# Attention with two mixtures of experts on one core: exponentials last in ScalarE's step, one scatter per step, a drain written out by hand

## The chip, the cores and the metric

The kernel runs on one core of a Trainium2 chip. The metric is the device time of one execution in microseconds (us), the median of several runs; the profile is of one further execution of the same program.

## The reference

Attention in a window of 128 positions with a linear bias per head, then a mixture of eight experts in which each token goes to the expert of its largest logit, then a mixture of four experts that every token visits:

```python
# q, k, v: 4 x 8 heads x 576 x 64
scores = q @ k.T / sqrt(64) + slope[head] * -abs(rel)      # rel = query position - key position
mask = (rel >= 0) & (rel < 128)
attn = softmax(where(mask, scores, -1e9)); x = attn @ v    # -> 2304 rows of 512
# mixture 1: 8 experts, w1 512x1024, w2 1024x512
e = argmax(x @ w_gate); x = gate[e] * relu(x @ w1[e]) @ w2[e]
# mixture 2: 4 experts
out = sum_e p[:, e] * (relu(x @ w1[e]) @ w2[e])
```

## The kernel before

The 2304 rows are 18 tiles of 128 (`NTT`). **Attention** goes over 36 steps s (`ns`), two per tile: step s handles tile t = s // 2 and four of its eight heads. It is a pipeline of three steps' depth, and everything is issued in the order in which the Python loop of lines 700 to 753 writes it; each engine takes its own instructions in that order. In step s:

- `st_qk(s)`: TensorE writes the bias (L418) and the scores (L426, each operand in a high and a low part) of this step.
- `st_max(s)`: ScalarE copies half the scores out (L436), VectorE takes the maximum with the other half (L437) and the row maxima `nm` (L442).
- `st_turn(s-2)`: TensorE transposes the probabilities of two steps ago (L459), ScalarE copies them to SBUF (L461), GpSimd cuts them into two triangles (L468: the window's part in this tile and in the one before).
- `st_exp(s)`: ScalarE takes four exponentials (L449), which wait for `nm`.
- `st_vw(t)` in odd steps: TensorE multiplies the values by the gate's weights (L540).
- `st_pv(s-3)`: TensorE multiplies the triangles by the values (L480, 16 matmuls); `st_row(s-3)`: VectorE divides by the sums (L505 to L527), and after a tile's second half adds up the gate's logits (L552).
- then the splits of coming keys and queries into high and low parts (`split_k`, `split_q`: ScalarE L246 or L258, VectorE L247 or L259), builds of two further bias tables in the first eleven steps (L304, ScalarE, up to three per step), and in six of the steps the high and low part of one weight tile (L134 on ScalarE, L138 on VectorE in the next step).

**Routing** is done by groups of tiles (`CUTS`: 0-2, 3-5, 6-8, 9-11, 12-13, 14-15, 16, 17). When a group's logits are there, a generator (`st_route`) is queued in `back`; each call of `route_op` issues its next small piece. VectorE finds the expert of each row (L573 to L588), TensorE counts the ranks (L593 to L599; the `yield "rank"` holds it back for the head of a step), VectorE makes the row numbers (L610), and GpSimd scatters each tile's rows to DRAM with an indirect DMA (L625), all tiles of a group one after the other. A second generator (`gates`, from `gate_of`) makes the gate's softmax in five pieces, ahead of any later group. The groups below `LATE` (tiles 0 to 15) are the early ones. After the last of them the first expert's rows so far are read back as `early` (L633). Tiles 16 and 17 reach the first expert by matmuls with a placement matrix (`put`, L653) instead.

The **drain** is three further turns of the same loop: s = 36, 37 and 38 issue the last transposes and products; in turn 38 the rest of tile 16's routing and the transposes of the first `early` tile (`first_rows(0)`, L644) stand ahead of the last product. `first_chunk` then adds the other early tiles, tiles 16 and 17, and splits the result (L185) for the first expert.

The **two mixtures** follow, from the first matmul in L789 to the end.

Of the kernel before, what the change touches and what calls it, by code (L numbers as in the profile page):

```python
# [14 lines left out]
ALU = mybir.AluOpType  # L15
# [35 lines left out]
def kernel(  # L51
# [153 lines left out]
    def attention():  # L205
        actx = ExitStack()
        with actx:
# [94 lines left out]
            def build_bias(x, h, o, w):  # L302
                slope = 2.0 ** (-8.0 * (h + 1) / H)
                nc.scalar.activation(  # L304
                    out=biases[x][:, h, o:o + w], in_=rels[x][:, 0:w], func=AF.Copy, scale=-slope
                )
# [253 lines left out]
            def st_route(g):  # L560
# [29 lines left out]
                if t0 < LATE:  # L590
                    yield "rank"
# [32 lines left out]
                for j, t in enumerate(tiles):  # L624
                    nc.gpsimd.indirect_dma_start(  # L625
# [32 lines left out]
            def first_chunk():  # L658
                first_rows(1, 2)
# [27 lines left out]
            held = []  # L687

            def route_op(rank=False):
                todo = gates if gates and (not back or gates[0][0] < back[0][0]) else back  # L690
                if not todo or (held and not rank):
                    return
                held.clear()
                got = next(todo[0][1], "end")
                if got == "end":
                    todo.pop(0)
                elif got == "rank":
                    held.append(todo)

            for s in range(ns + 3):  # L700
# [5 lines left out]
                if s < ns:  # L706
                    st_qk(s)
                    if s == 1:
                        busy(ps_t, "t", 4)
                    st_max(s)  # L710
                if 2 <= s < ns + 2:
                    st_turn(s - 2)
                if s < ns:
                    st_exp(s)
                route_op(rank=True)
                if s == ns + 2:
                    while back:
                        route_op(rank=True)
                    first_rows(0)
                if hf == 1 and s < ns:  # L720
                    st_vw(t)
# [3 lines left out]
                if s == ns + 2:  # L725
                    break
# [3 lines left out]
                if s < ns:  # L730
                    if hf == 0:
                        if 2 <= t + 1 < NTT:
                            split_k(t + 1)
                        if t + 3 < NTT:
                            load(t + 3)
                    elif t + 2 < NTT:
# [651 lines left out]
```

## Time and profile before

| what | us |
|---|---|
| median of 3 runs (1188.45 to 1192.49) | 1188.8 |
| the profiled execution | 1188.37 |
| its span in the trace | 1185.7 |
| attention's steps 5 to 34 | 24.60 to 166.94 |
| step 35 and the drain, up to the first expert's first matmul | 166.94 to 194.86 |
| the two mixtures | 194.86 to 1185.7 |

To read it: TensorE is busy for nearly all of the span, so what counts is its clock and the time between its matmuls. "PEclk" is the granted clock of TensorE as a share of the full one: 1.00 is 2.4 GHz all the time, and a stretch at 1.2 GHz counts half. A table by stretches gives for each engine the busy time and the number of instructions. In a timeline each row is a start, a duration, an engine, a source line, an operation and its tiles; a bracket tells how long the engine had been idle before it and who ended the wait. A name with a prefix of a queue (SPq) is a DMA's issue.

### The profile page before, as it was taken

The numbers are of one execution on the slowest core, as the hardware profiler recorded it, in microseconds if no ns is written. First come the engines' busy times: TensorE is split into PE (matmuls) and PEld (weight loads), VectorE is DVE, ScalarE is ACT, GpSimd is POOL, SyncE is SP. The second block draws the span as 40 slices with busy tenths as digits, with TensorE's granted clock in tenths as the row PEclk, the third lists the DMA queues.
The fourth block names the chain that finished last, engine by engine and source line by source line (L and its number), as shares of the span: only waits on it lengthen the run. The fifth ranks groups of instructions, "written<-read, shape, count | busy, mean of one in ns | idle before, by whom it ended". The sixth has DMA issues, their size and how long they took to land.

```text
span 1185.7 us, 17746 instructions
## 1 busy us (share of the span) xinstructions
PE 1157.8 (98%) x6785; PEld 1057.4 (89%) x6786; DVE 773.0 (65%) x1428; ACT 527.5 (44%) x988; POOL 112.3 (9%) x158
## 2 busy tenths in 40 slices
PE   8999997999999999999999999999999999999997
PEld 5787887999999998999999899999999899999996
DVE  4678774465575466666666876666667866666663
ACT  5776652454465453333333443333334433333331
POOL 3244341001310000000000100000000200000001
PEclk9799898999999999999999999999999999999999
DMA  9556423455575413211122322112212322222201
GB/s 328 189 162 213 157 76 126 154 191 168 156 216 166 141 44 101 65 57 59 70 72 71 103 93 72 63 63 71 72 58 67 125 72 71 71 72 71 72 18 53
DMA packets 62225, 126.58 MB, mean 107 GB/s; under 512 B 26272, under 2 KB 26272, under 8 KB 62112
## 3 DMA queue, kind: packets, MB, share of 16 engines
q1 hardware_dynamic: 58368, 114.96, 30.5%
q0 software_dynamic: 3456, 9.51, 2.0%
q8 instruction: 79, 1.29, 0.5%
q10 hardware_dynamic: 288, 0.52, 0.1%
q14 instruction: 34, 0.28, 0.1%
HBM read 109.18 MB, written 15.80 MB: 105 GB/s over the span
## 4 chain that ended last, share of the span: by engine, by line
issue 71%; PE 20%; POOL 3%; DVE 3%; ACT 2%; DMA 1%; POOLq 0%; ACTq 0%; SPq 0%; DVEq 0%
PE g L789 6%; PE y L894 6%; PE xo L480 3%; PE sc L426 2%; POOL out_dram L1319 2%; ACT pr L449 1%; PE pt L459 1%; PE sc L418 1%; DVE nm L442 1%; PE vw L540 1%; POOL pt L468 1%; DVE pr L437 1%; PE xps L861 1%; POOL xs L625 0%; ACT pr L436 0%
## 5 line engine op out<-in xcount | busy, mean ns | idle before, releaser
L138 DVE TENSOR_TENSOR wlo<-raw,whi 128x1024 fp32r<-128x1024 f32 x160 | 193.4, 1221 | 130.1 <-ACT whi L134 128.5
L1298 PE MATMUL l<-whi,hhi 128*128 128x512 f32 x576 | 224.5, 390 | 1.6 <-DVE acc L1315 1.6
L1298 PE MATMUL l<-whi,hlo 128*128 128x512 f32 x576 | 224.9, 390 | 0.0
L1298 PE MATMUL l<-wlo,hhi 128*128 128x512 f32 x576 | 224.8, 390 | 0.0
L134 ACT CAST whi<-raw 128x1024 fp32r<-128x1024 f32 x160 | 165.4, 1053 | 130.9 <-DVE raw L160 106.0
L1211 ACT COPY x<-X 128x384 f32<-128x384 f32 x126 | 60.4, 480 | 269.2 <-PE X L1190 269.2
L1315 DVE SCALAR_TENSOR_TENSOR acc<-l,ct,acc 128x512 f32<-128x512 f32 x126 | 94.2, 748 | 81.7 <-PE l L1298 81.7
L1298 PEld LDWEIGHTS l<-whi,hhi 128*128 128x128 f32 x576 | 108.2, 188 | 24.4 <-DVE acc L1315 2.5
L1298 PEld LDWEIGHTS l<-whi,hlo 128*128 128x128 f32 x576 | 108.2, 188 | 22.5
L1298 PEld LDWEIGHTS l<-wlo,hhi 128*128 128x128 f32 x576 | 108.2, 188 | 21.9
L1319 POOL DMA_INDIRECT out_dram<-acc,ctok x18 | 22.2, 1236 | 818.0 <-DVE acc L1315 488.2
L1216 DVE TENSOR_TENSOR x<-Z,x 128x384 f32<-128x384 f32 x84 | 44.7, 554 | 67.5 <-ACT x L1211 67.5
L480 PE MATMUL xo<-vr,pt 128*128 128x73 f32 x544 | 74.4, 292 | 3.6 <-POOL pt L468 2.0
L480 PEld LDWEIGHTS xo<-vr,pt 128*128 128x128 f32 x544 | 69.6, 206 | 5.9 <-POOL pt L468 5.9
L1222 ACT ACTIVATE hhi<-x 128x384 fp32r<-128x384 f32 x126 | 58.1, 520 | 30.9 <-DVE x L1216 30.9
L894 PE MATMUL y<-hhi,whi 128*128 128x256 f32 (+2 forms) x224 | 69.7, 311 | 1.0 <-issue 1.0
L894 PE MATMUL y<-hlo,whi 128*128 128x256 f32 (+2 forms) x224 | 69.1, 309 | 0.0
L894 PE MATMUL y<-hhi,wlo 128*128 128x256 f32 (+2 forms) x224 | 68.9, 307 | 0.0
L1228 DVE SCALAR_TENSOR_TENSOR hlo<-x,hhi 128x384 fp32r<-128x384 f32 x126 | 62.8, 553 | 2.7
L449 ACT ACTIVATE pr<-pr,nm 128x128 f32<-128x128 f32 x128 | 40.9, 390 | 39.1 <-DVE nm L442 39.1
L777 ACT ACTIVATE hhi<-g 128x384 fp32r<-128x384 f32 x64 | 31.1, 492 | 49.8 <-PE g L789 45.0
L778 DVE SCALAR_TENSOR_TENSOR hlo<-g,hhi 128x384 fp32r<-128x384 f32 x64 | 35.1, 554 | 27.3 <-ACT hhi L777 23.7
(354 smaller groups left out, 2595.1 us busy)
## 6 DMA issues: line engine op xcount, KB each, us to landing
raw<-in_w_b_dram SPq DMA_DIRECT2D x96, 512.0 KB, 3.6
raw<-in_w_a_dram SPq DMA_DIRECT2D x64, 512.0 KB, 3.8
xs<-zrow SPq DMA_DIRECT2D x8, 768.0 KB, 6.4
row<-xs SPq DMA_DIRECT2D x7, 768.0 KB, 5.5
rk<-in_k_dram SPq DMA_DIRECT2D x18, 256.0 KB, 4.2
vr<-in_v_dram SPq DMA_DIRECT2D x18, 256.0 KB, 3.4
rv<-in_vt_dram SPq DMA_DIRECT2D x18, 256.0 KB, 3.4
rq<-in_q_dram SPq DMA_DIRECT2D x16, 256.0 KB, 4.4
```

The costliest lines, as they stand in the source:

```text
L134: nc.scalar.copy(out=hi, in_=src)
L138: nc.vector.tensor_tensor(out=lo, in0=src, in1=hi.bitcast(F32), op=ALU.subtract)
L449: nc.scalar.activation(out=pr[:, r, jj, :], in_=scores[:, r, jj, :], func=AF.Exp, bias=nm[:, r, jj:jj + 1], scale=1.0,)
L480: nc.tensor.matmul(xo[:, i, :], pt[c][:, i, :], vr[:, c % NSLOT, 4 * hf + i, :], start=(n == 0), stop=(n == len(pt) - 1),)
L789: nc.tensor.matmul(ps[:, 0:w], wl[:, c0:c0 + P], xl[dt // 2][:, dt % 2, 0:w], start=(dt == 0 and n == 0), stop=(dt == NDT - 1 and n == 2),)
L894: nc.tensor.matmul(acc[:, 0:w], wl[:, c0:c0 + P], hl[:, 0:w], start=(f == 0 and x == 0), stop=(f == NFT - 1 and x == 2),)
L1211: nc.scalar.copy(out=to, in_=xb[i])
L1222: nc.scalar.activation(out=hi, in_=c, func=AF.Relu)
L1228: nc.vector.scalar_tensor_tensor(out=lo, in0=c, scalar=0.0, in1=hi.bitcast(F32), op0=ALU.max, op1=ALU.subtract)
L1298: nc.tensor.matmul(acc, hl[:, ts], wl[:, c0:c0 + DM], start=(m == 0 and x == 0), stop=(m == 3 and x == 2),)
L1315: nc.vector.scalar_tensor_tensor(out=accs[g], in0=acc, scalar=pe, in1=accs[g], op0=ALU.mult, op1=ALU.add)
L1319: nc.gpsimd.indirect_dma_start(out=outv[g], out_offset=bass.IndirectOffsetOnAxis(ap=ctok[:, g, :], axis=0), in_=accs.pop(g), in_offset=Non ...
```

## The change

It moves work in attention's loop and in the drain; nothing that is computed changes.

1. `st_exp(s)` is issued behind the splits of keys and queries and the bias builds instead of ahead of them, though still ahead of a weight tile's high part. The builds of the two further tables for odd heads go to VectorE (12 of 40; eight of 128x256 or 128x128 elements for one table, four of 128x256 for the other).
2. The generator of a group stops ("hold") ahead of the rank matmuls, as before, and also ahead of each scatter, and goes on at the head of a step, behind that step's transposes and triangles. Groups of two tiles hold once for both scatters, and the last early group does not hold there.
3. The gate's softmax is issued only while the group's generator holds, or when there is none.
4. The last early group (tiles 14 and 15): its pieces up to the hold are all issued in step 34, and in step 35 the rank matmuls and the next piece, with the scatters and the reads of `early`, follow at once.
5. The drain is written out. The last transposes, products and routing pieces stand in their own order, the rest of tile 16's routing ahead of the last product, and all transposes of `early` (`first_rows(0, 1, 2)`) behind it.

```diff
             def build_bias(x, h, o, w):
...
+                if x and h % 2:
+                    nc.vector.tensor_scalar(out=out, in0=rels[x][:, 0:w], scalar1=-slope, scalar2=None, op0=ALU.mult)
+                else:
+                    nc.scalar.activation(out=out, in_=rels[x][:, 0:w], func=AF.Copy, scale=-slope)
...
                 if t0 < LATE:
-                    yield "rank"
+                    yield "hold"
...
                 for j, t in enumerate(tiles):
+                    if t0 < OPEN and (j == 0 or m > 2):
+                        yield "hold"
                     nc.gpsimd.indirect_dma_start(
...
             def first_chunk():
-                first_rows(1, 2)
+                first_rows(*range(TT))
...
+            def route_op(head=False):
+                if gates and not head and (waiting or not back):
+                    if next(gates[0][1], "end") == "end":
+                        gates.pop(0)
+                elif back and (head or not waiting):
+                    waiting.clear()
+                    got = next(back[0][1], "end")
+                    if got == "end":
+                        back.pop(0)
+                    elif got == "hold":
+                        waiting.append(got)
+
+            for s in range(ns):
...
+                if s >= 2:
                     st_turn(s - 2)
-                if s < ns:
-                    st_exp(s)
-                route_op(rank=True)
...
+                route_op(head=True)
+                if s == 2 * LATE + 3:
+                    route_op()
...
                 route_op()
+                st_exp(s)
                 if late:
                     late.pop(0)()
                 if s in SPLITS:
                     w_split(late)
                 route_op()
+                while s == 2 * LATE + 2 and not waiting:
+                    route_op()
+            st_turn(ns - 2)
+            st_pv(ns - 3)
+            st_row(ns - 3)
+            for _, steps in gates:
+                for _ in steps:
+                    pass
+            st_turn(ns - 1)
+            for _ in range(4):
+                route_op()
+            st_pv(ns - 2)
+            st_row(ns - 2)
+            while back:
+                route_op(head=True)
+            st_pv(ns - 1)
+            st_row(ns - 1)
```

ScalarE in steps 6 and 7 (`pr` are the probabilities, `pt` the transposed ones, `khi` and `qhi` the keys' and queries' high parts), before:

```order
L436 COPY pr_561<-sc_546 128x512
L461 COPY pt_571<-pt_566 128x512
L449 ACTIVATE pr_561<-pr_561,nm_564 128x128 x4
L246 CAST khi<-rk_332 128x4x128
L304 ACTIVATE bias_179<-rel_161 128x256 x3
L134 CAST whi_609<-raw_403 128x1024
L436 COPY pr_627<-sc_612 128x512
L461 COPY pt_637<-pt_632 128x512
L449 ACTIVATE pr_627<-pr_627,nm_630 128x128 x4
L258 ACTIVATE qhi_669<-rq_470 128x512
L304 ACTIVATE bias_179<-rel_161 128x256 x3
```

and now:

```order
L438 COPY pr_561<-sc_546 128x512
L463 COPY pt_571<-pt_566 128x512
L246 CAST khi<-rk_328 128x4x128
L308 ACTIVATE bias_179<-rel_161 128x256 x2
L451 ACTIVATE pr_561<-pr_561,nm_564 128x128 x4
L134 CAST whi_609<-raw_399 128x1024
L438 COPY pr_627<-sc_612 128x512
L463 COPY pt_637<-pt_632 128x512
L258 ACTIVATE qhi_665<-rq_466 128x512
L308 ACTIVATE bias_179<-rel_161 128x256
L451 ACTIVATE pr_627<-pr_627,nm_630 128x128 x4
```

The exponentials moved behind the split and the bias builds of their step, and of the six builds three went to VectorE.

GpSimd where the first group's three tiles are scattered (L468 and L470 are the triangles, two per step; the names with a higher number are later steps), before:

```order
L468 AFFINE_SELECT pt_0_843<-pt_841 128x512
L468 AFFINE_SELECT pt_1_845<-pt_841 128x512
L625 DMA xs<-xrow_392,row_i 18433x512
L625 DMA xs<-xrow_529,row_i 18433x512
L625 DMA xs<-xrow_662,row_i 18433x512
L468 AFFINE_SELECT pt_0_924<-pt_922 128x512
L468 AFFINE_SELECT pt_1_926<-pt_922 128x512
```

and now:

```order
L470 AFFINE_SELECT pt_0_844<-pt_842 128x512
L470 AFFINE_SELECT pt_1_846<-pt_842 128x512
L470 AFFINE_SELECT pt_0_917<-pt_915 128x512
L470 AFFINE_SELECT pt_1_919<-pt_915 128x512
L629 DMA xs<-xrow_388,row_i 18433x512
L470 AFFINE_SELECT pt_0_986<-pt_984 128x512
L470 AFFINE_SELECT pt_1_988<-pt_984 128x512
L629 DMA xs<-xrow_525,row_i 18433x512
L470 AFFINE_SELECT pt_0_1051<-pt_1049 128x512
L470 AFFINE_SELECT pt_1_1053<-pt_1049 128x512
L629 DMA xs<-xrow_658,row_i 18433x512
```

The three scatters stood ahead of one step's triangles; now each stands behind the triangles of its own step.

GpSimd from step 35 on (the first pair of triangles is that of step 33's probabilities, then those of 34 and 35; the scatters are those of tiles 14, 15 and 16), before:

```order
L468 AFFINE_SELECT pt_0_2499<-pt_2497 128x512
L468 AFFINE_SELECT pt_1_2501<-pt_2497 128x512
L468 AFFINE_SELECT pt_0_2540<-pt_2538 128x512
L468 AFFINE_SELECT pt_1_2542<-pt_2538 128x512
L625 DMA xs<-xrow_2267,row_i 18433x512
L625 DMA xs<-xrow_2406,row_i 18433x512
L468 AFFINE_SELECT pt_0_2592<-pt_2590 128x512
L468 AFFINE_SELECT pt_1_2594<-pt_2590 128x512
L625 DMA xs<-xrow_2523,row_i 18433x512
```

and now:

```order
L470 AFFINE_SELECT pt_0_2498<-pt_2496 128x512
L470 AFFINE_SELECT pt_1_2500<-pt_2496 128x512
L629 DMA xs<-xrow_2254,row_i 18433x512
L629 DMA xs<-xrow_2392,row_i 18433x512
L470 AFFINE_SELECT pt_0_2559<-pt_2557 128x512
L470 AFFINE_SELECT pt_1_2561<-pt_2557 128x512
L470 AFFINE_SELECT pt_0_2588<-pt_2586 128x512
L470 AFFINE_SELECT pt_1_2590<-pt_2586 128x512
L629 DMA xs<-xrow_2537,row_i 18433x512
```

The scatters of the last early group moved ahead of step 34's triangles, one step up.

## Rows read from the trace of the kernel before

**Rows 1.** The page: TensorE's granted clock in 40 slices of the span

```profile
PEclk9799898999999999999999999999999999999999
```

**Rows 2.** Table by stretches: length, each engine's busy time, clock, DMA share, GB/s

```profile
24.60:60.19 35.59, 32.49 (x236) 27.16 (x236) 22.59 (x60) 26.06 (x74) 8.51 (x15) 0.81 0.60 205
60.19:90.66 30.47, 30.06 (x279) 25.77 (x278) 24.42 (x73) 21.84 (x53) 13.60 (x18) 1.00 0.57 174
90.66:115.34 24.68, 23.45 (x220) 20.06 (x220) 19.66 (x60) 16.45 (x42) 8.20 (x11) 1.00 0.66 213
115.34:132.44 17.10, 15.53 (x112) 12.97 (x112) 11.43 (x31) 8.78 (x22) 6.99 (x10) 0.80 0.32 108
132.44:166.94 34.50, 34.04 (x318) 29.20 (x318) 27.58 (x88) 23.56 (x59) 15.29 (x20) 1.00 0.51 160
166.94:194.86 27.92, 20.27 (x141) 18.89 (x141) 15.40 (x64) 7.45 (x21) 9.01 (x12) 0.82 0.18 65
194.86:1185.70 990.84, 979.75 (x5364) 908.93 (x5364) 640.98 (x1033) 410.14 (x685) 42.56 (x38) 1.00 0.29 92
```

**Rows 3.** Timeline of TensorE: first matmul of steps 14, 15, 16 and 17

```profile
73.88 0.59 PE L418 MATMUL sc<-bias,identb 128*128 128x512 bf16 x2
...
77.55 0.59 PE L418 MATMUL sc<-bias,identb 128*128 128x512 bf16 x2
...
82.11 0.59 PE L418 MATMUL sc<-bias,identb 128*128 128x512 bf16 x2
...
86.10 0.59 PE L418 MATMUL sc<-bias,identb 128*128 128x512 bf16 x2
```

**Rows 4.** Timelines of ScalarE, and of TensorE for the last row, in the early steps

```profile
31.18 0.56 ACT L436 COPY pr<-sc 128x512 f32<-128x512 f32 x1
31.64 0.57 ACT L461 COPY pt<-pt 128x512 f32<-128x512 f32 x1
33.21 1.28 ACT L449 ACTIVATE pr<-pr,nm 128x128 f32<-128x128 f32 x4 [1.00 <-DVE nm L442]
34.40 0.61 ACT L258 ACTIVATE qhi<-rq 128x512 fp32r<-128x512 f32 x1
34.92 0.91 ACT L304 ACTIVATE bias<-rel 128x128 bf16<-128x128 f32 x3
35.73 0.56 ACT L436 COPY pr<-sc 128x512 f32<-128x512 f32 x1
...
42.44 0.66 PE L459 MATMUL pt<-ident,pr 128*128 128x128 f32 x4 [0.98 <-ACT pt L461]
```

**Rows 5.** Timelines of GpSimd and TensorE at the third group's scatters

```profile
113.93 0.98 POOL L625 DMA_INDIRECT xs<-xrow,row_i  x1 [1.20 <-DVE base L611]
...
118.14 1.25 POOL L468 TENSOR_SCALAR_AFFINE_SELECT pt<-pt 128x512 f32<-128x512 f32 x2
...
118.86 3.82 PE L480 MATMUL xo<-vr,pt 128*128 128x73 f32 x16 [1.43 <-POOL pt L468]
...
122.48 1.06 PE L418 MATMUL sc<-bias,identb 128*128 128x512 bf16 x2
```

**Rows 6.** Timelines of the drain: VectorE, GpSimd, SyncE's queue and TensorE

```profile
177.77 0.97 POOL L625 DMA_INDIRECT xs<-xrow,row_i  x1 [0.30 <-issue]
...
180.53 1.28 SPq L633 DMA_DIRECT2D early<-xs  x3
...
183.13 1.12 PE L644 MATMUL xps<-ident,early 128*128 128x128 f32 x4 [4.11 <-DMA early<-xs]
184.04 3.53 PE L480 MATMUL xo<-vr,pt 128*128 128x73 f32 x16
...
187.60 0.16 DVE L505 TENSOR_SCALAR den<-xo 128x4 f32<-128x4 f32 x1 [6.59 <-PE xo L480]
...
191.26 0.42 DVE L616 TENSOR_SCALAR put<-slot,row_f 128x384 fp32r<-128x384 f32 x1
...
194.86 0.41 PE L789 MATMUL g<-x0('s', 0)_0_2707,whi 128*128 128x384 f32 x1 [1.39 <-ACT x0('s', 0)_1_2708 L185]
```

More of the change, by code (lines that the diff above doesn't have):

```diff
@@ L303, in build_bias @@
                 slope = 2.0 ** (-8.0 * (h + 1) / H)
-                nc.scalar.activation(
-                    out=biases[x][:, h, o:o + w], in_=rels[x][:, 0:w], func=AF.Copy, scale=-slope
-                )
+                out = biases[x][:, h, o:o + w]
+                if x and h % 2:
+                    nc.vector.tensor_scalar(out=out, in0=rels[x][:, 0:w], scalar1=-slope, scalar2=None, op0=ALU.mult)
+                else:
+                    nc.scalar.activation(out=out, in_=rels[x][:, 0:w], func=AF.Copy, scale=-slope)
             for h in range(H):
@@ L685, in attention @@
             back, late, consts, extra = [], [], late_consts(), late_biases()
[L687 to L700, printed above, removed]
+            waiting = []
+            def route_op(head=False):
[10 more added lines that the diff above has]
+            for s in range(ns):
                 t, hf = divmod(s, 2)
@@ L705, in attention @@
                     busy(ps_t, "t", 3)
-                if s < ns:
[L707 to L711, printed above, removed]
-                    st_turn(s - 2)
-                if s < ns:
-                    st_exp(s)
-                route_op(rank=True)
[L716 to L720, printed above, removed]
+                st_qk(s)
+                if s == 1:
+                    busy(ps_t, "t", 4)
+                st_max(s)
+                if s >= 2:
+                    st_turn(s - 2)
+                route_op(head=True)
+                if s == 2 * LATE + 3:
+                    route_op()
+                if hf == 1:
                     st_vw(t)
@@ L724, in attention @@
                     st_row(s - 3)
-                if s == ns + 2:
-                    break
                 if hf == 0 and 2 <= t + 1 < NTT:
@@ L729, in attention @@
                 route_op()
[L730 to L736, printed above, removed]
-                        split_q(t + 2)
-                    if s == 1:
-                        row_consts()
-                    if s in (3, 5):
-                        w_dma(nxt["dma"])
-                    if s < E1:
-                        clear_rows(s)
-                    if s == 20:
-                        domain_probs()
-                    for todo in (consts, consts, extra, extra, extra):
-                        next(todo, None)
+                if hf == 0:
+                    if 2 <= t + 1 < NTT:
+                        split_k(t + 1)
+                    if t + 3 < NTT:
+                        load(t + 3)
+                elif t + 2 < NTT:
+                    split_q(t + 2)
+                if s == 1:
+                    row_consts()
+                if s in (3, 5):
+                    w_dma(nxt["dma"])
+                if s < E1:
+                    clear_rows(s)
+                if s == 20:
+                    domain_probs()
+                for todo in (consts, consts, extra, extra, extra):
+                    next(todo, None)
                 route_op()
+                st_exp(s)
                 if late:
```

## The prediction

> **What bounds the kernel now.** I read the page's slices of TensorE's clock first, then a table by stretches, then the timelines of the engines where TensorE waits. The slices [rows 1] show one clock nearly everywhere, with lower digits only in the first fifth. So the table [rows 2] cuts that fifth by steps: 24.60 to 60.19 is steps 5 to 10, then 11 to 17, 18 to 23, 24 to 26, 27 to 34, then step 35 with the drain, then the mixtures. The last row says that nothing is to be had in the mixtures: 979.75 of 990.84 us busy at a clock of 1.00, and the change leaves them alone. In attention the clock is 0.81 in steps 5 to 10, 0.80 in steps 24 to 26, 0.82 in the drain and 1.00 elsewhere.
>
> What a step costs when TensorE waits for nobody is read from the starts of four steps in a row [rows 3]: 77.55 - 73.88 = 3.67 us for an even one, 82.11 - 77.55 = 4.56 for an odd one (it has the values' matmuls too), 86.10 - 82.11 = 3.99 for an even one with rank matmuls, so these cost 0.32. Clean lengths of the stretches follow by counting: steps 5 to 10 take 3 x 4.56 + 2 x 3.67 + 3.99 = 25.01, steps 11 to 17 29.57, steps 24 to 26 11.90, steps 27 to 34 (two rank steps) 33.56. Steps 18 to 23 would take 25.01 too, but two of them have 8 of the 16 products; 16 took 3.53 at the lower clock [rows 6], which is 1.77 at the full one, so two halves less make 23.2. Against the table this leaves 10.6, 0.9, 1.5, 5.2 and 0.9 us lost, 19.1 in all, of which the clock is (1 - 0.81) x 35.59 = 6.8 and 0.20 x 17.10 = 3.4.
>
> **ScalarE's order, edit 1.** In the early steps ScalarE runs a loop of its own, longer than TensorE's step [rows 4]: from one copy of scores at 31.18 to the next at 35.73 it is 4.55, against 4.11 for a clean step on average ((3.67 + 4.56) / 2). In it are 1.00 of waiting for the row maxima, 34.40 - 33.21 = 1.19 of exponentials, and 1.33 of split and bias builds behind them. At 42.44 TensorE's transposes wait 0.98 for ScalarE's copy, and the clock of the stretch is 0.81. With the exponentials last, split and builds fill the wait: the maxima are there 33.21 - 31.18 = 2.03 after the copy starts, and copy, copy, split and one or two builds take at most 2.1, so the loop is about 2.1 + 1.19 = 3.3, well under 4.11. The exponentials come no later than some 5 us after their step's start, and the transposes want them two steps on, at 8.2 + 1.4; that is the cover, and it is some 4 us wide. A weight tile's high part still fits on top in one step of five. So the 10.6 of steps 5 to 10 is open to be had. What is late next is VectorE: 22.59 busy there, plus four of the twelve builds. The nearest row for a build there is 0.42 for 128x384 of the same kind [rows 6]; a build has 128 to 256 columns, so it costs between nothing and 0.42. 22.59 + 4 x 0.42 = 24.3 of 25.01 is tight for an engine that must wait for products in order. In steps 11 to 17 it reaches a share of 24.42 / 30.47 = 0.80, and at no more than that the stretch would need 24.3 / 0.80 = 30.4. So the waits that stay are between 0 and 5.4; I take 1.5, nearer to 0 because steps 11 to 17 run almost clean at that share: -9.1. Two builds also stand ahead of tile 1's keys at the start, before step 2: at most 2 x 0.42, I take +0.3.
>
> **One scatter per step, edit 2.** Where a group is scattered, GpSimd does three of them from 113.93 on, and the next triangles start at 118.14 only; TensorE's products wait 1.43 for them, run 3.82 in place of 1.77, and the next bias matmuls at 122.48 still take 1.06 where a clean step has 0.59 [rows 3, 5]: TensorE was granted 1.2 GHz. Now each scatter stands behind triangles that are wanted a step later, and 0.98 of scatter with 1.25 of triangles is far below a step. This takes the 5.2 of steps 24 to 26 (3.4 of it clock), the 0.9 of steps 11 to 17 and the 0.9 of steps 27 to 34. Of the 1.5 in steps 18 to 23 I take half, 0.7 (ends 0 and 1.5): VectorE is busy for 19.66 of 23.2 there. A new wait enters in step 33: the rank matmuls of tiles 12 and 13 moved from step 32 to 33, and their one-hot rows are now written behind that step's key split on VectorE, so TensorE reaches them first. The two nearest rows for such a wait are 0 and 1.43; I take 0.5. Holding scatters back delays nobody else, as the `early` rows depend on the last early group.
>
> Together: -9.1 + 0.3 - 0.9 - 0.7 - 5.2 - 0.9 + 0.5 = **-16.0 us** up to step 35.
>
> **The last early group and the drain, edits 4 and 5.** From 166.94 to 194.86 it is 27.92, TensorE busy 20.27 at a clock of 0.82 [rows 2]: 20.27 x 0.82 = 16.6 of work at the full clock, 3.7 lost to the clock, 7.6 idle. The longest wait is 4.11, for the reads of `early`, up to 183.13; behind it stand the last product, at the lower clock, and everything that hangs on it: VectorE's chain from 187.60 over the placement matrix at 191.26 to 194.86 [rows 6]. The reads left at 180.53 and wait for the scatters, which started last at 177.77. In the new order the rank matmuls stand in step 35, where they were in the step after, so the scatters come about four us earlier, and `early` is wanted later, behind the last product. 183.13 - 4 is before that product's end, so this wait goes. What stays: the wait of 1.39 for the split at 194.86, and VectorE's chain between the last product and the placement, 191.26 - 187.60 = 3.66, of which TensorE covers a part with tile 16 and `early`. So between 1.4 and 1.4 + 3.7 = 5.1 of waits; I take 3.6, since the chain gets one more wait, for the one-hot rows in step 35. Length 16.6 + 3.6 = 20.2, a gain of 7.7 at the full clock. But most of these waits lie close together at the very end, as the waits did at 118.86, so I let the clock fall once for the price that it had there, 3.4: **-4.3 us**, ends -9.9 (27.92 - 16.6 - 1.4) and 0.
>
> The Trainium skill's page TensorE: Matmul & The Clock Gate, in A second HAM failure mode: psum-queue depth-cycling, says that short idles between groups of matmuls can make the clock swing between its two states, at a cost between the bursts. That speaks against a drain of many short waits: at the present 0.82 over the whole of it the loss would be 5.0 and the sum 1169.7. The rows of steps 24 to 26 agree that a wait of 1.43 is enough.
>
> **Sum.** The profiled execution took 1188.37 us (its span 1185.7 and 2.7 around it), 0.4 under the median. 1188.4 - 16.0 - 4.3 = **1168.1**.
>
> **Rivals.** (B) VectorE becomes the bound in steps 5 to 10. For it: 24.3 of 25.01; against it: the builds are small and its waits for ScalarE go. Then TensorE idles there as now, the clock falls as now, and 6.8 of clock and 1 of waits come back: 1176. (C) The drain gains nothing: two scatters now stand ahead of step 34's triangles, and if VectorE's row numbers come a step late, these, the products and the chain wait. For it: VectorE writes its row numbers behind other work; against: nothing else is then queued on GpSimd. 1168.1 + 4.3 = 1172. (D) The change doesn't do what it says: ScalarE's 1.00 of waiting only moves behind the split, and its loop stays at 4.5. Against it: 1.33 of work now lies inside the wait. 1168.1 + 9.1 = 1177. (E) Slower: maxima, exponentials, next copy, next maxima are a ring over VectorE and ScalarE, and since the exponentials are last in their step, whatever makes VectorE late makes the next copy late. VectorE's busy time over steps 5 to 34 is 105.7 [rows 2], 3.5 a step; it decides from when its need passes the 4.74 (142.3 / 30) that a step takes now, that is with 1.2 of waits a step. Then TensorE idles in every step and the clock is 0.81 throughout: 0.19 x 142.3 = 27 lost in place of 10.2, less the drain's gain: 1201. Against it: today's waits of VectorE are mostly for ScalarE.
>
> **How the numbers follow.** The forecast (1160 to 1171) 0.55; C 0.13; B and D 0.18; nothing to be measured 0.08 (several of these at once); E 0.06. The range reaches from the ends of the terms (19.1 + 9.9 = 29 less: 1159.4) over C, B and D: 1160 to 1179. A measurement of this kernel can tell about 0.5% (5.9 us) from no change: faster 0.55 + 0.13 + 0.18 = 0.86, same 0.08, slower 0.06.
>
> **What would show it.** Steps 5 to 10 take about 26.5 at a clock of 0.95 or more, and ScalarE's brackets name no maxima; if B or D holds, the stretch stays above 32 and the brackets tell which engine. No product waits for triangles behind a scatter; a bracket of over 1 us there means edit 2 failed. TensorE's rank matmuls in steps 33 and 35 show brackets of about half a us. `early` lands before the last product ends, and the drain takes 20 to 24; a bracket of `early` over 1 us is C. The mixtures keep 991; if they move by over 2 us, what I left out was wrong.

## The result, and the profile after

The changed kernel takes 1159.91 us (median of 6 runs, 1159.48 to 1161.58), the kernel before 1187.26 beside it (6 runs, 1185.42 to 1192.49): a ratio of 0.9768, 95% interval 0.9747 to 0.979. The prediction's 1168.1 had the direction and was 8 us too high; the time lies just under its range of 1160 to 1179. The ends of the prediction's terms come to 1159.4, which it rounded up to 1160. The profiled execution fell from 1188.37 to 1159.63 us, its span from 1185.7 to 1157.9.

TensorE's clock on the page, and the table by the same stretches as in [rows 2] (length; busy time of TensorE, its weight loads, VectorE, ScalarE, GpSimd; granted clock; DMA share; GB/s):

```profile
PEclk8999999999999999999999999999999999999999
```

```profile
24.15:49.16 25.01, 25.01 (x236) 21.66 (x236) 21.86 (x64) 22.25 (x61) 8.80 (x15) 1.00 0.83 289
49.16:78.73 29.57, 29.57 (x279) 25.66 (x279) 23.84 (x73) 23.06 (x55) 12.20 (x19) 1.00 0.58 178
78.73:101.98 23.25, 22.91 (x220) 19.95 (x220) 18.86 (x60) 16.21 (x40) 7.47 (x10) 1.00 0.69 228
101.98:113.87 11.89, 11.89 (x112) 10.22 (x112) 10.48 (x30) 8.44 (x21) 7.39 (x11) 1.00 0.47 156
113.87:147.73 33.86, 33.69 (x317) 29.14 (x317) 27.97 (x87) 24.66 (x58) 13.27 (x20) 1.00 0.47 149
147.73:166.59 18.86, 16.84 (x142) 15.15 (x141) 14.47 (x65) 7.87 (x20) 10.14 (x13) 1.00 0.35 125
166.59:1157.90 991.31, 979.85 (x5364) 908.76 (x5364) 640.24 (x1033) 410.32 (x685) 43.37 (x38) 1.00 0.29 92
```

From step 5 to the first expert the clock is 1.00 in every row, and in three of the attention's rows TensorE's busy time is the row's whole length. Ahead of step 5, in the start, the granted clock was 0.79 (1.00 in the kernel before), and the start is not longer for it. Against [rows 2] and the prediction's terms, in us:

| stretch | before | after | change | forecast |
|---|---|---|---|---|
| start, up to step 5 | 24.60 | 24.15 | -0.45 | +0.3 |
| steps 5 to 10 | 35.59 | 25.01 | -10.58 | -9.1 |
| steps 11 to 17 | 30.47 | 29.57 | -0.90 | -0.9 |
| steps 18 to 23 | 24.68 | 23.25 | -1.43 | -0.7 |
| steps 24 to 26 | 17.10 | 11.89 | -5.21 | -5.2 |
| steps 27 to 34 | 34.50 | 33.86 | -0.64 | -0.4 |
| step 35 and drain | 27.92 | 18.86 | -9.06 | -4.3 |
| mixtures | 990.84 | 991.31 | +0.47 | 0 |
| around the span | 2.67 | 1.73 | -0.94 | 0 |
| sum | | | -28.74 | -20.3 |

ScalarE in steps 6 and 7, the rows that answer to [rows 4] (start, duration, engine, line, operation, tiles; in brackets the idle time before it and who ended it):

```profile
30.31 0.59 ACT L438 COPY pr<-sc 128x512 f32<-128x512 f32 x1 [0.53 <-PE sc L428]
31.40 0.62 ACT L246 CAST khi<-rk 128x512 fp32r<-128x512 f32 x1
31.92 0.72 ACT L308 ACTIVATE bias<-rel 128x256 bf16<-128x256 f32 x2
32.54 1.26 ACT L451 ACTIVATE pr<-pr,nm 128x128 f32<-128x128 f32 x4
33.71 1.03 ACT L134 CAST whi<-raw 128x1024 fp32r<-128x1024 f32 x1
34.65 0.57 ACT L438 COPY pr<-sc 128x512 f32<-128x512 f32 x1
```

The split and the builds fill what was a wait of 1.00 for the maxima, and a weight tile's high part fits on top. ScalarE's loop now follows TensorE's steps (five of its steps, from the copy at 26.43 to that at 46.77, take 20.34 us, 4.07 each) and waits for TensorE's scores. Other steps of the stretch still have brackets for the maxima, of 0.16 to 0.71 us, so the prediction's sign (none of them) was too strict; they reach no TensorE instruction. GpSimd at the third group, for [rows 5]:

```profile
103.35 0.98 POOL L629 DMA_INDIRECT xs<-xrow,row_i  x1 [0.16 <-issue]
105.86 1.21 POOL L470 TENSOR_SCALAR_AFFINE_SELECT pt<-pt 128x512 f32<-128x512 f32 x2 [1.53 <-PE xo L482]
107.24 0.99 POOL L629 DMA_INDIRECT xs<-xrow,row_i  x1 [0.17 <-issue]
```

One scatter per step, and before the next step's triangles GpSimd itself waits. The drain, for [rows 6]; these are TensorE's brackets from step 33 to the first expert, with the transposes of `early`, which have none:

```profile
141.28 0.17 PE L599 MATMUL rkp<-oh_all,tri 128*128 128x24 bf16 x1 [0.17 <-DVE oh_all L590]
150.26 0.17 PE L599 MATMUL rkp<-oh_all,tri 128*128 128x24 bf16 x1 [0.30 <-issue]
159.81 1.80 PE L648 MATMUL xps<-ident,early 128*128 128x128 f32 x12
163.47 0.41 PE L657 MATMUL xps<-put,rowhi 128*128 128x384 f32 x1 [0.20 <-DVE put L618]
166.59 0.41 PE L804 MATMUL g<-x0('s', 0)_0_2707,whi 128*128 128x384 f32 x1 [1.47 <-ACT x0('s', 0)_1_2708 L185]
```

In the kernel before, tile 16's ranks had waited too, just ahead of the 4.11 for `early`:

```profile
178.82 0.17 PE L597 MATMUL rkp<-oh_all,tri 128*128 128x16 bf16 x1 [1.62 <-DVE oh_all L588]
```

The 4.11 for `early` and the 1.62 for tile 16's one-hot rows are gone. `early` comes just in time: TensorE's weight loads wait 0.16 and 0.20 us for it, its matmuls not at all. For the 0.30 at 150.26 the profile names no releaser ("issue"); in n_again (experiment 3) the same bracket names the one-hot rows. From step 35 on the brackets make 0.30 + 0.20 + 1.47 = 1.97 of the 2.02 that the table leaves idle.

### The profile page after: what moved, and what is told of

Read it like the earlier page. It is cut to its first block, busy times and chain, and to the rows that moved or that the text cites. A ratio compares the mean times of both kernels' runs of the same rounds, so it can differ in the third digit from the quotient of the medians.

```text
span 1157.9 us, 17740 instructions
## 1 busy us (share of the span) xinstructions
PE 1141.1 (99%) x6785; PEld 1044.3 (90%) x6786; DVE 771.2 (67%) x1440; ACT 527.5 (46%) x976; POOL 110.7 (10%) x158
## 4 chain that ended last, share of the span: by engine, by line
issue 71%; PE 25%; POOL 2%; DVE 1%; DMA 0%; POOLq 0%; ACT 0%; ACTq 0%
PE g L804 6%; PE y L909 6%; PE xo L482 5%; PE sc L428 3%; POOL out_dram L1334 2%; PE pt L461 2%; PE vw L542 1%; PE sc L420 1%; PE xps L876 1%; DMA rk<-in_k_dram 0%; DVE klo L247 0%; PE xps L657 0%; PE idle L104 0%; PE xps L648 0%; DVE qlo L259 0%
## 5 line engine op out<-in xcount | busy, mean ns | idle before, releaser
L482 PE MATMUL xo<-vr,pt 128*128 128x73 f32 x544 | 66.8, 275 | 0.2 <-PE vw L542 0.2
L482 PEld LDWEIGHTS xo<-vr,pt 128*128 128x128 f32 x544 | 63.7, 192 | 0.3 <-issue 0.3
L470 POOL TENSOR_SCALAR_AFFINE_SELECT pt<-pt 128x512 f32<-128x512 f32 x64 | 41.3, 669 | 85.2 <-ACT pt L463 80.7
```

What stands on the lines that cost most here:

```text
L482: nc.tensor.matmul(xo[:, i, :], pt[c][:, i, :], vr[:, c % NSLOT, 4 * hf + i, :], start=(n == 0), stop=(n == len(pt) - 1),)
```

## Experiments

**1. Each edit alone, on the kernel before.** b_exp moves only the exponentials:

```diff
-                if s < ns:
-                    st_exp(s)
                 route_op(rank=True)
...
                 route_op()
+                if s < ns:
+                    st_exp(s)
                 if late:
```

> The kernel before with one half of edit 1: the exponentials are the last thing of ScalarE's step (ahead of a weight tile's high part only); all bias builds stay on ScalarE. Theory (a stretch is clean only if no engine's need passes TensorE's): ScalarE was busy for 26.06 us in steps 5 to 10, of which the changed kernel moved 3.8 us to VectorE (22.25 there); with all of it on ScalarE its need is over the 25.01 us that TensorE needs, so the order alone leaves the stretch between 26.5 and 31 us, with some waits of TensorE for ScalarE's copies and a clock below 1.00 in parts. Rival (the order was all, the moved builds gave nothing): 25.0 to 25.5 us at a clock of 1.00. Either way steps 24 to 26 keep about 17 us and the drain about 28.

b_edit1 adds the twelve builds on VectorE (the change's piece in `build_bias`):

> The kernel before with edit 1 whole (exponentials last, 12 builds on VectorE) and nothing else. Theory (each edit repairs its own stretch and nothing else): steps 5 to 10 take 25.0 us at a clock of 1.00, a gain of 10.6 us, the start some 0.3 to 0.5 us less; steps 24 to 26 keep 17 us and the drain 28; in all about 11 us less than before, ratio 0.991. Rival (the exponentials' place also frees the triangles and the drain, by keeping the engines ahead): steps 24 to 26 fall to 12 us too, and the gain is 16 us or more, ratio 0.986.

b_hold has `yield "rank"` ahead of a scatter, as edit 2, and the old `route_op`:

```diff
                 for j, t in enumerate(tiles):
+                    if t0 < OPEN and (j == 0 or m > 2):
+                        yield "rank"
                     nc.gpsimd.indirect_dma_start(
```

> The kernel before with edit 2 alone: a hold ahead of each scatter, so that one scatter stands behind a step's triangles; exponentials, builds, last early group and drain as before. Theory: steps 24 to 26 take 11.9 us at a clock of 1.00 (5.2 less), the brackets of 0.27 and 0.32 us behind other scatters go (0.9 each in steps 11 to 17 and 27 to 34), steps 18 to 23 lose some of their 1.5; steps 5 to 10 keep 35 to 36 us, the drain 28: a gain of 6 to 8 us, ratio 0.994. Rival (the scatters were not what held the triangles up; with the exponentials ahead the wait at the third group comes from the late copy of the transposed probabilities): steps 24 to 26 stay above 15 us, ratio 0.998 or more.

b_drain is the changed kernel with edits 1 and 2 taken out:

> The kernel before with edits 3, 4 and 5 alone: the last early group routed at once, its ranks and scatters in step 35, the drain written out; exponentials, builds and scatters as before. Theory (the drain's gain stands by itself; the reads of early come ahead of the last product, and without a wait of microseconds the clock stays at 1.00): step 35 with the drain takes 18.5 to 20 us in place of 27.9, the stages before it as before; a gain of 8 to 9 us, ratio 0.9925. Rival (the drain was cheap in the changed kernel only because the exponentials and scatters before it had been put in order): 22 to 25 us with a clock below 1.00, gain 3 to 5 us, ratio 0.996.

Measured beside 25 runs of the kernel before (median 1185.0, 1180.36 to 1191.96):

| kernel | median us | runs from, to | ratio | 95% interval |
|---|---|---|---|---|
| b_exp | 1176.81 | 1173.16, 1180.53 | 0.9935 | 0.9912 to 0.9958 |
| b_edit1 | 1174.98 | 1172.82, 1180.74 | 0.9915 | 0.9879 to 0.9951 |
| b_hold | 1190.18 | 1184.83, 1196.38 | 1.0059 | 1.0025 to 1.0094 |
| b_drain | 1180.99 | 1173.38, 1187.31 | 0.9965 | 0.9934 to 0.9996 |

Steps 5 to 10 and 24 to 26 of b_exp, then the same of b_edit1:

```profile
24.43:49.44 25.01, 25.01 (x236) 21.66 (x236) 20.55 (x57) 23.49 (x66) 8.54 (x15) 1.00 0.83 285
104.25:121.40 17.15, 15.51 (x112) 12.95 (x112) 12.74 (x31) 9.33 (x24) 6.87 (x10) 0.80 0.32 108
```

```profile
26.02:51.03 25.01, 25.01 (x237) 21.66 (x237) 21.56 (x63) 22.06 (x60) 8.79 (x15) 1.00 0.81 272
105.82:119.82 14.00, 12.37 (x112) 10.31 (x112) 12.62 (x31) 9.22 (x24) 6.85 (x10) 1.00 0.39 132
```

The order alone makes steps 5 to 10 clean; the expectation that ScalarE's work would not fit was wrong (23.49 in 25.01; of the 3.8 us that it counted as builds only 23.49 - 22.25 = 1.24 were), and the rival was right that the builds give nothing there. b_edit1 came out at its expected ratio. Steps 24 to 26 hold a surprise: their order of instructions is the same in both kernels, and so are the waits, 1.04 or 1.03 and 0.60 for the triangles behind three scatters. TensorE in step 24 of b_exp and of b_edit1:

```profile
107.38 0.44 PE L480 MATMUL xo<-vr,pt 128*128 128x73 f32 x2 [1.04 <-POOL pt L468]
108.42 3.26 PE L480 MATMUL xo<-vr,pt 128*128 128x73 f32 x14 [0.60 <-POOL pt L468]
```

```profile
108.93 0.44 PE L482 MATMUL xo<-vr,pt 128*128 128x73 f32 x2 [1.03 <-POOL pt L470]
109.98 1.78 PE L482 MATMUL xo<-vr,pt 128*128 128x73 f32 x14 [0.60 <-POOL pt L470]
```

In one execution the products behind the waits run at 1.2 GHz (3.26), in the other at 2.4 (1.78), and the stretch differs by 17.15 - 14.00 = 3.15 us.

Edit 2 alone makes the kernel slower, where a gain of 6 to 8 us was expected. Its own stretch is repaired: no product waits for triangles in steps 24 to 26, which take 13.20 us in place of 17.10 (at a clock of 0.92, which fell just before, behind a wait of 1.84 for ScalarE's copy). But with the old `route_op` a hold stops everything behind it, the gate's pieces and the next group too, and the work piles up at the end. TensorE in the drain of b_hold, which takes 32.06 us there:

```profile
171.34 0.37 PE L593 MATMUL rkp<-base,top 128*128 128x24 f32 x2 [1.23 <-DVE sh L194]
173.08 0.17 PE L597 MATMUL rkp<-oh_all,tri 128*128 128x24 bf16 x1 [1.37 <-DVE oh_all L588]
180.61 1.12 PE L646 MATMUL xps<-ident,early 128*128 128x128 f32 x4 [5.86 <-DMA early<-xs]
```

The 1.23 names a piece of a gate's softmax (`sh`), but what this matmul reads is `base`, the running counts, which VectorE copied just ahead of that piece, at 171.03 (L611): two groups' ranks now stand one behind the other in the drain. The 5.86 (4.11 before) is for the reads of `early` behind them. The profiled execution took 1184.83 us, the fastest of the eight; what makes others up to 12 us longer no trace shows.

In b_drain the drain took 24.71 us, with brackets of 0.30, 0.20 and 1.48 as in the changed kernel, but at a clock of 0.72: the rival's numbers, by a cause of its own (experiment 3). Step 35 with the drain in b_drain:

```profile
167.49:192.20 24.71, 22.73 (x142) 21.50 (x141) 14.29 (x63) 7.86 (x20) 8.16 (x11) 0.72 0.22 74
```

Nor did the stages ahead of it keep their length, though nothing in them was meant to change: steps 5 to 10 took 29.97 us at a clock of 0.94 (35.59 at 0.81 before), steps 24 to 26 20.23 at 0.66 (17.10 at 0.80). What the old order costs differs from one execution to the next.

So the edits do not add up: 10.0 less, 5.2 more and 4.0 less than 1185.0 make 8.8 less; all of them together give 25 to 27.

**2. One part undone in the changed kernel.** a_self is the changed kernel itself. In a_noexp edit 1 is undone, in a_nohold the hold ahead of the scatters, in a_d4 the early routing of tiles 14 and 15:

```diff
-                if s == 2 * LATE + 3:
-                    route_op()
...
-                while s == 2 * LATE + 2 and not waiting:
-                    route_op()
             st_turn(ns - 2)
+            route_op(head=True)
             st_pv(ns - 3)
             st_row(ns - 3)
+            route_op()
```

> The changed kernel itself, beside the kernels of which one part is undone, to see how far its own runs lie apart. Theory (the runs of the other kernels lie up to 14 us apart because a wait of about a microsecond on TensorE makes its clock fall in some executions and not in others; the changed kernel has no such wait before the first expert, so it has nothing to fall): ratio 0.977 to 0.980, its own runs within 3 us of each other. Rival (the spread is the machine's, whatever the kernel): its runs lie as far apart as those of before, 8 us or more.

> The changed kernel with edit 1 undone: exponentials ahead of the splits and builds again, all builds on ScalarE; holds, gates, last early group and drain as changed. Theory 1 (edits add up, each in its own stretch): steps 5 to 10 back to 30 to 35.6 us, everything else as in the changed kernel; 5 to 11 us over it, ratio 0.983 to 0.989. Theory 2 (the holds need edit 1: with the exponentials ahead of the split, whatever is late reaches TensorE through ScalarE's copy): waits for ScalarE's copies also in later steps (18 to 26), and falls of the clock there: 13 us or more over the changed kernel, ratio 0.990 or more.

> The changed kernel with edit 2 undone: no hold ahead of a scatter, so that a group's scatters stand together ahead of a step's triangles. Theory: TensorE waits for triangles behind them as in the kernel that had edit 1 alone, 0.27 to 1.6 us at each of the five groups, 3.1 in all, and 0 to 3.2 us of clock for each group where it falls: 3 to 8 us over the changed kernel, ratio 0.980 to 0.985, and runs that lie 5 us or more apart. Rival (with edit 1 and edit 3 in place the triangles have a step's time, and the scatters cost nothing): within 1 us of the changed kernel.

> The changed kernel with edit 4 undone: tiles 14 and 15 are routed at the pace of the loop again, their ranks in the first turn behind step 35 and their scatters and the reads of early behind that turn's products, 4 to 5 us later; the drain's other order stays. Theory (early is in its place just in time in the changed kernel, TensorE's weight loads wait 0.4 us for it): a bracket of 3 to 5 us for early behind the last product, drain 22 to 24 us, and the clock falls in addition in some runs (up to 3.4 us more): ratio 0.981 to 0.985. Rival (the order of edit 5 alone hides it): bracket under 1 us, drain under 20 us.

In a_d5 the first early tile's transposes stand ahead of the last product again:

```diff
+            first_rows(0)
             st_pv(ns - 1)
...
-                first_rows(*range(TT))
+                first_rows(1, 2)
```

> The changed kernel with one piece of edit 5 undone: the transposes of the first early tile stand ahead of the last product again, those of the other two behind it; the last early group is still routed at once. Theory (early lands just in time for its place behind the last product: there its weight loads waited 0.4 us at 159.7): TensorE comes to it 1.7 us sooner, waits 1.5 to 2 us, and the cover behind the last product is a third shorter: drain 20.4 to 21.5 us at a clock of 1.00, 23 to 25 where the clock falls; 2 to 6 us over the changed kernel, ratio 0.981 to 0.985. Rival (the order of the drain is worth nothing once the reads are early): drain 18.5 to 19 us, within 1 us of the changed kernel.

The first four ran beside 13 runs of the kernel before (median 1185.7, 1180.34 to 1191.29), a_d5 beside 7 (1185.47):

| kernel | median us | runs from, to | ratio | 95% interval |
|---|---|---|---|---|
| a_self | 1160.2 | 1158.03, 1160.72 | 0.9803 | 0.9762 to 0.9844 |
| a_noexp | 1181.24 | 1172.66, 1187.82 | 0.9949 | 0.9912 to 0.9987 |
| a_nohold | 1166.58 | 1164.51, 1168.07 | 0.9864 | 0.9823 to 0.9906 |
| a_d4 | 1166.23 | 1164.19, 1168.17 | 0.986 | 0.9817 to 0.9902 |
| a_d5 | 1162.08 | 1160.28, 1164.46 | 0.9816 | 0.9789 to 0.9844 |

Without edit 1 the kernel loses 21 us, twice what edit 1 gave alone: theory 2's number. Steps 5 to 10 take 35.30 us again, but not as before: TensorE waits there once, for 0.77, and the rest of the loss is the clock.

```profile
24.12:59.42 35.30, 34.53 (x237) 29.60 (x236) 22.34 (x59) 24.89 (x69) 8.51 (x15) 0.71 0.58 203
26.40 0.66 PE L459 MATMUL pt<-ident,pr 128*128 128x128 f32 x4 [0.77 <-ACT pt L461]
```

In the later steps, though, the waits are not for ScalarE's copies: TensorE's rank matmuls wait for the one-hot rows. With the exponentials ahead of the split, VectorE waits for ScalarE's high parts (0.90 at 151.85, 0.28 at 156.53) and then writes these rows too late. The first row is VectorE's in a_noexp, then TensorE's behind it:

```profile
151.85 0.69 DVE L259 SCALAR_TENSOR_TENSOR qlo<-rq,qhi 128x512 fp32r<-128x512 f32 x1 [0.90 <-ACT qhi L258]
```

```profile
157.36 0.17 PE L597 MATMUL rkp<-oh_all,tri 128*128 128x24 bf16 x1 [2.02 <-DVE oh_all L588]
158.32 3.57 PE L480 MATMUL xo<-vr,pt 128*128 128x73 f32 x16
```

a_self came out as the theory had it, with runs 2.7 us apart where those of before lie 11 apart. a_nohold has nearly the waits of b_edit1, 2.8 us for triangles, and lies 6.4 over a_self, as expected; steps 24 to 26 take 14.00, and its runs lie closer together (3.6) than expected. a_d4 came out near the expected total (ratio 0.986, expected 0.981 to 0.985) by other rows than expected. There is no bracket for `early`; the later ranks and scatters make TensorE wait at three places, and the product behind the third ran at 1.2 GHz (drain 23.89 at a clock of 0.86):

```profile
154.21 0.17 PE L599 MATMUL rkp<-oh_all,tri 128*128 128x24 bf16 x1 [0.73 <-DVE oh_all L590]
159.68 0.17 PE L599 MATMUL rkp<-oh_all,tri 128*128 128x16 bf16 x1 [1.03 <-DVE oh_all L590]
160.90 3.97 PE L482 MATMUL xo<-vr,pt 128*128 128x73 f32 x16 [1.03 <-POOL pt L470]
```

In a_d5 the transposes wait 1.18 for `early` (theory: 1.5 to 2), the drain takes 20.06 at a clock of 1.00, and the time lies about 2 us over a_self. So this piece of edit 5 is worth 1.2 us in the trace and about 2 by the medians, which is not clear of the noise, and the early routing of edit 4 about 6, some of it clock. Edit 3 and the rest of edit 5 were not undone by themselves.

**3. Does the clock fall in every execution?** a_nodve and n_again are one program: the changed kernel with all bias builds on ScalarE. n_rank and a_rank put the value matmuls ahead of the rank matmuls in odd steps, to take away the last wait ahead of the drain, n_rank in that program and a_rank in the changed kernel:

```diff
+                if hf == 1:
+                    st_vw(t)
                 route_op(head=True)
                 if s == 2 * LATE + 3:
                     route_op()
-                if hf == 1:
-                    st_vw(t)
```

> The changed kernel with the twelve bias builds back on ScalarE; the exponentials stay last. Theory (with the order alone steps 5 to 10 of the kernel before took 25.01 us, so ScalarE's 23.5 us of work fits, and the builds gave nothing): within 1 us of the changed kernel, steps 5 to 10 take 25.0 us. Rival (the medians of the two kernels with edit 1 alone, 1176.8 without the builds on VectorE and 1175.0 with them, show a real gain): 1.5 to 2 us over the changed kernel.

> The same kernel as a_nodve (the changed kernel with all bias builds on ScalarE), run more often. Theory (the fall of the clock in the drain behind the rank matmuls' wait of 0.31 us comes in some executions of one program and not in others): about half of the runs near 1160 us, the others near 1167 us, and few between. Rival (the builds' place makes the kernel slower in every run): the runs lie within 3 us of each other, 1.5 us or more over the changed kernel's 1160.

> The kernel of n_again, in which the value matmuls of an odd step are issued ahead of the rank matmuls instead of behind them, so that VectorE has 0.8 us more to write the one-hot rows. Theory (the wait of 0.31 us in step 35 is what lets the clock fall in the drain): the brackets of 0.17 and 0.31 us in steps 33 and 35 are gone, all runs lie near 1160 us (1158 to 1161), none near 1167. Rival (the fall has nothing to do with that wait): as many runs near 1167 us as in n_again.

> The changed kernel with the value matmuls ahead of the rank matmuls in odd steps, as in n_rank. Theory: the brackets of 0.17 and 0.30 us go, everything else stays: 0.3 to 0.6 us under the changed kernel (1159.4 against 1160), all runs within 3 us; a version a little better than both kernels or the same. Rival (the later rank matmuls make the scatters and the reads of early late): the brackets come back at the transposes of early, 1 us or more over the changed kernel.

a_nodve ran beside the same 7 runs of the kernel before as a_d5, the others beside 11 (median 1183.38):

| kernel | median us | its runs | ratio | 95% interval |
|---|---|---|---|---|
| a_nodve | 1163.57 | 1159.08, 1160.30, 1166.84, 1167.09 | 0.9812 | 0.9772 to 0.9851 |
| n_again | 1159.25 | six, 1158.79 to 1160.86 | 0.9794 | 0.9759 to 0.983 |
| n_rank | 1162.37 | six, 1160.37 to 1163.74 | 0.9821 | 0.9785 to 0.9857 |
| a_rank | 1161.56 | six, 1160.74 to 1163.57 | 0.9813 | 0.9776 to 0.9849 |

One program, and ten runs: eight near 1160 and two near 1167. The two profiles of it show steps 5 to 34 alike to 0.01 us per stretch, the same bracket in step 35, and then this. First step 35 with the drain in a_nodve and two of its rows, then step 35 with the drain in n_again and the same bracket:

```profile
148.18:174.44 26.26, 24.35 (x142) 23.13 (x141) 14.43 (x65) 7.79 (x20) 10.14 (x13) 0.68 0.24 88
```

```profile
150.72 0.17 PE L597 MATMUL rkp<-oh_all,tri 128*128 128x24 bf16 x1 [0.31 <-DVE oh_all L588]
153.91 1.06 PE L459 MATMUL pt<-ident,pr 128*128 128x128 f32 x4
```

```profile
147.76:166.50 18.74, 16.72 (x142) 15.17 (x141) 14.50 (x65) 7.87 (x20) 10.13 (x13) 1.00 0.35 126
```

```profile
150.29 0.17 PE L597 MATMUL rkp<-oh_all,tri 128*128 128x24 bf16 x1 [0.30 <-DVE oh_all L588]
```

In a_nodve the transposes at 153.91 run at 1.2 GHz (1.06 for what takes 0.60), and the drain takes 26.26 - 18.74 = 7.52 us more. The clock falls in some executions of one program and not in others, with no wait to tell them apart. So the builds' place does not make it fall in every run (n_again); whether it changes the chance these runs don't tell. Nor do they tell whether the chip matters: a_nodve's four runs, two of each kind, were on one chip, n_again's six on another.

Whether the wait of 0.30 starts it stays open. For it speaks the place: in the drains of b_drain and a_noexp the clock fell there too, 2 to 3 us behind the same bracket (0.30 and 0.31) as in a_nodve. Against it, the two profiles of the changed kernel, n_again, a_nohold and a_d5 have that bracket at 0.30 or 0.31, a_load1 at 0.41, and kept 2.4 GHz. n_rank and a_rank take it away and no run of theirs is near 1167, but none of n_again's was either, so they don't tell. What they do show is the rival of a_rank: with the rank matmuls 0.8 us later `early` comes too late, and TensorE waits for it. TensorE in the drain of a_rank, which takes 20.35:

```profile
161.95 1.31 PE L648 MATMUL xps<-ident,early 128*128 128x128 f32 x8 [0.66 <-DMA early<-xs]
163.88 0.66 PE L648 MATMUL xps<-ident,early 128*128 128x128 f32 x4 [0.62 <-DMA early<-xs]
```

What is won ahead of the drain (0.34 in steps 27 to 34) is lost behind it, and no version here beats the changed kernel by what can be measured.

**4. How much room has VectorE?** a_load1 and a_load3 add one and three instructions to VectorE's step:

```diff
+                for _ in range(1 if s > 4 else 0):
+                    nc.vector.tensor_scalar(out=idle[:, 0:2 * P], in0=rels[0][:, 0:2 * P], scalar1=1.0, scalar2=None, op0=ALU.mult)
```

> The changed kernel with one more instruction of VectorE in each step from step 5 on, a scaled copy of 128x256 like the bias builds, 0.28 us each; it goes to a tile that nobody reads afterwards. VectorE's need in steps 5 to 34 rises from 103.0 to 111.4 of 123.6 us. Theory (VectorE has room, and the exponentials' place leaves some 4 us of it before the transposes): within 2 us of the changed kernel. Rival (whatever is added to VectorE reaches TensorE, since VectorE works in order): over 5 us slower, with brackets for ScalarE's copies or for row sums in most steps.

> The changed kernel with three such instructions of VectorE in each step from step 5 on, 0.84 us in all: its need in steps 5 to 34 is 128.2 us, more than TensorE's 123.6. Theory (the slower case of the prediction: from there TensorE waits in every step, and the clock falls with the waits): 20 to 35 us over the changed kernel, the clock in steps 5 to 34 at 0.8 to 0.9. Rival (only the surplus counts): 5 to 8 us over it at a clock near 1.00.

a_load1: 1160.21 us (1160.03 to 1168.75), ratio 0.9819, 0.9776 to 0.9863; three of four runs are at the changed kernel's time, and the fourth, which was not profiled, is 8.5 over them at a lower clock. a_load3: 1196.35 (1192.72 to 1201.96), ratio 1.0106, 1.0064 to 1.0148. VectorE was busy for 108.4 and 128.0 us in steps 5 to 34 (111.4 and 128.2 expected). So one more instruction is free but for that one run, of which it is not shown whether the instruction brought it, and three cost 36 us, a little over the theory's 35. But not as the prediction's rival E would have it: up to step 9 the steps of a_load3 keep their clean length, and TensorE waits first at the rank matmuls, at five places for 10.4 us in all, with the clock lost behind them. The first of the five, and the products and the next step behind it:

```profile
51.64 0.18 PE L599 MATMUL rkp<-oh_all,tri 128*128 128x32 bf16 x1 [2.63 <-DVE oh_all L590]
51.75 3.35 PE L482 MATMUL xo<-vr,pt 128*128 128x73 f32 x16
54.90 1.06 PE L420 MATMUL sc<-bias,identb 128*128 128x512 bf16 x2
```

## Why the prediction was too high

**The drain: right mechanism, mis-sized (4.8 of the 8.4 us).** The prediction put 16.6 of work, 3.6 of waits and 3.4 of clock; measured were 16.84, 2.02 and none. The failed step is "so I let the clock fall once for the price that it had there, 3.4". It took the clock's fall for certain and for one price. The runs show it as a matter of chance: none in the two profiles of the changed kernel's drain and, as its ten runs lie within 3.6 us, none of this size in any of them; two falls in the ten runs of the program that differs only in the builds' place, of 7.5 us in the one that was profiled. 3.4 is neither. With such a fall the changed kernel would have come to about 1167 (an estimate, 1159.9 + 7.5), near the forecast, so how far off it was is in part chance; the term's ends, -9.9 and 0, hold the measured -9.06. The 3.6 of waits were 1.6 too many: the chain behind the last product was kept at 3.66 with part of it bare, but the twelve transposes, tile 16's placement and tile 17's ranks cover all but 0.20.

**Steps 5 to 10 (1.5 us).** "The waits that stay are between 0 and 5.4; I take 1.5": they are 0. VectorE is busy for 21.86 of 25.01 us (the prediction's 24.3 was too much), a share of 0.87, and TensorE waits nowhere, so the 0.80 of steps 11 to 17 was no limit; a_load1 puts still more on it (22.38). Rivals B and D are out, and with no bracket for `early` on TensorE's matmuls C is too. Of the 10.58 gained, 6.8 was clock, which differs from one execution to the next with the old order (29.97 us in b_drain). That the moved builds were needed was wrong in the other direction: b_exp does without them.

**Smaller terms.** The start gained 0.45 where 0.3 more was feared; that says little, since a_self, the same program, has a start of 24.53 in place of 24.15. Steps 18 to 23 gave all of their 1.5, the rank wait in step 33 is 0.17 (0.5 forecast; 0.30 in step 35), and 0.94 lies outside the span. The mixtures moved by 0.47, within the 2 us allowed.

**Edit 2.** The 5.2 of steps 24 to 26 came to 0.01 us, but it was partly luck: b_exp and b_edit1 show that the 3.4 of clock in it comes or not with the same waits. "The rows of steps 24 to 26 agree that a wait of 1.43 is enough" is true of that execution; in b_edit1 1.03 and 0.60 were not. And "Holding scatters back delays nobody else" is false with the old `route_op`, where a hold delays the gates and everything behind (b_hold, 0.6% slower); in the changed kernel it holds. Which of edits 3 and 4 it needs was not tested.

**Adding up.** The sum assumed that each edit repairs its own stretch. In the traces the waits that an edit aims at do go (25.01 us in steps 5 to 10 of b_exp and b_edit1, no triangles waited for in steps 24 to 26 of b_hold, the changed kernel's brackets in b_drain's drain). But by themselves the edits gave 8.8 us in place of 25 to 27, as new waits came in or the clock fell all the same, and edit 1 undone costs 21 us where it gave 10.0 alone. A wait left in one stretch can lose the clock there and make the next engine late; that this is the whole difference is not shown, with one profiled execution of each kernel.

**A drain of short waits** was also weighed by the Trainium skill, TensorE: Matmul & The Clock Gate, section A second HAM failure mode: psum-queue depth-cycling: 1169.7 by it. The changed kernel does not agree (clock 1.00 with 0.30, 0.20 and 1.47 of waits); a_nodve does (0.68 with 0.31, 0.20 and 1.40). The same page of the Trainium skill says in What's actually happening that at a kernel's start the point at which the clock rises varies from run to run of one kernel. Experiment 3 shows a difference between runs of one program too, but for a fall in the middle of it, and at 7.5 us.

## What to carry to other kernels

A wait of a microsecond or less ahead of TensorE is priced as its length plus a chance of a fall of the clock, which here cost 3 us in steps 24 to 26 of b_exp, 7.5 in the drain of a_nodve and some 10 in steps 5 to 10 of a_noexp (0.29 x 35.30); so sum such a term with both ends, and don't take one profiled execution's fall for a fixed cost. A wide spread of the runs is a sign of such waits: 12 us before (25 runs), under 4 after (10 runs). A narrow one is no proof against them: a_nohold's four runs lie 3.6 apart with 2.8 us of waits. And try edits of one pipeline together and by undoing them one at a time: by themselves they may show a fraction of their worth, or the wrong sign.

## What was not expected of the hardware

TensorE's clock fell at one instruction in one execution and not in another, with the same waits ahead of it: 1.04 and 0.60 us in step 24 (3.26 against 1.78 us for 14 products), 0.31 and 0.30 in step 35 (a drain of 26.26 against 18.74). In a_nodve no wait above 0.31 us stood in the 50 us ahead of the fall, and matmuls ran at 1.2 GHz from 153.91 on, though TensorE was busy for 24.35 of the stretch's 26.26 us. What decides when it falls is not shown by these runs.
